# Asking for the convolution's taps first, straight to 128 partitions

## The chip, the cores and the metric

The kernel runs on one core of one Trainium2 chip. The metric is the device time of one execution in microseconds (us): the median of the runs of one kernel. Below, TensorE is the matrix engine (PE for its matmuls, PEld for its weight loads), VectorE is DVE, ScalarE is ACT, GpSimd is POOL, and SyncE is SP. ACT, SP and POOL can also ask for DMA transfers; all of these share the core's 16 DMA engines.

## The reference

Two layers. The first is a causal convolution along the sequence with softmax-normalised taps: 8 heads of 24 channels, 7 taps each. The second is a feed-forward layer with a ReLU gate.

```python
B, S, D = 8, 4096, 192;  H, K = weight.shape      # 8 heads, 7 taps
w = exp(weight - max(weight, axis=-1));  w = w / (sum(w, axis=-1) + 1e-9)
out[b, s, h, :] = sum over k of w[h, k] * x[b, s + k - 6, h, :]      # zero ahead of the sequence
x = out.reshape(32768, 192)
gate = maximum(x @ moe_w_gate, 0);  val = x @ moe_w_val              # 192 -> 1536
result = (gate * val) @ moe_w_out                                     # 1536 -> 192
```

## The kernel before, in words

**Tiles and units.** The batch of 8 sequences is cut into two halves ("streams"), worked side by side: channels 64c to 64c + 63 (c = 0, 1, 2) of stream 0 lie in partitions 0 to 63 and those of stream 1 in 64 to 127. A unit is 1024 tokens of both streams; there are 16 units, each two windows of 512 tokens. For each window, `gate_val` runs over 12 slices f of 128 hidden channels: matmuls with `Wg` and `Wv` (L560), a ReLU on ACT (L571), a product on DVE (L572). `project_turn` then does the last matmul with `Wo` (L582).

**The convolution** is done in two ways. For units 2 to 15, a "lane" of products and sums on ACT, DVE and POOL makes `xc`, using `tap`, a table with one column of 7 taps for each channel. For units 0 and 1 there is no time for that, so TensorE does it: a band matrix per head, 118 rows by 112 tokens, with the 7 taps on its diagonals. `conv_steps` (L372 to L394) takes the first 512 tokens in five steps jj of 112 tokens, for each of the three channel groups c.

**The start**, with which the change is concerned, runs in this order:
- `early` (L129) makes ACT load its exponential table.
- `w8` (L131) asks for the taps as an 8 x 7 tile on ACT's queue. `load_raw` asks for the five blocks of x: jj = 1, 0, 3, 4 on SP's queue, jj = 2 on ACT's (L132 to L134).
- POOL makes `ones`, then by affine selects `rows8` (1 where partition h belongs to head h's 16 columns, L156) and the identity `eye` (L158), then clears `Z` and the first rows of x block 0.
- DVE sums `eye` into `Z` (L164: which of 16 offsets within a head a partition stands for) and `mask` (L170: which head it belongs to). A one-element memset of `Wg` on DVE (L180) is what POOL's first weight request waits for.
- TensorE runs matmuls on constants (`hold`, L195) whose results nobody reads, in counts of 128 columns from `WARM`. Between them stands one matmul of value, L205: `rows8` by `w8` gives `spread`, the taps of head p // 16 in each of 128 partitions. Three matmuls by zeros (L211) clear the PSUM areas in which the bands will be built.
- From `spread`: the negated maximum `mx` on DVE (L285), the exponential `e` on ACT (L288), its sum `sm` (L291), then `prod`, `blk`, the reciprocal and `blocks` on DVE (L297 to L309). Eight matmuls for each of three groups of heads (L330) lay the blocks on the diagonals, and DVE copies the bands out (L338).
- ACT casts the five blocks of x to 16 bits (L121), in the order 1, 0, 2, then the normalised taps `wn` (L318), then 3, 4. They feed the convolution (L386) with the bands; `evict` (L397) writes `xc` for the first 512 tokens, and L560 begins.

**The weights** come by eight requests on POOL's queue (`load_w`, L226: columns cut at 128, 384, 768), into partitions 0 to 63. The upper half is a copy of the lower (`both_halves`, L233), slice by slice: 0 and 1 by DVE, 2 to 9 by POOL (`pool_halves`), 10 (the last 256 columns) by DMA. POOL's queue holds, in this order: the eight requests, copies of slice 2, a load of x, slices 3 to 5, a load of x, slices 6 and 7, a load of x, slices 8 and 9.

**The order of work** on each engine is that of the program text (`manual_schedule`), and each engine takes its queue in order. `psum` has four buffers, used in rotation; `spread` takes one of them. The table `tap` is filled by 20 small DMAs on SP's queue from `wn` (L349), which reads 8 partitions that hold the taps of head h: before, 16h to 16h + 7.

Of the kernel before, what the change touches and what calls it, by code (L numbers as in the profile page):

```python
# [8 lines left out]
FP = mybir.dt.float32  # L9
F16 = mybir.dt.float16  # L10
ACTF = mybir.ActivationFunctionType
ALU = mybir.AluOpType
# [3 lines left out]
def kernel(  # L16
# [12 lines left out]
    nc = tc.nc  # L29

    B, S, D = x.shape
    H, KW = weight.shape
# [10 lines left out]
    STEPS = [6, 5, 2]  # L43
    TAPS = [(6, 5), (4, 3), (2, 1, 0)]
    GSUB = 5
    WARM = [(4, 4, 4, 1), (4, 4, 1)]
    STEPS0 = [1, 0, 2, 3, 4]
    CONV1 = 10

# [12 lines left out]
    const = ctx.enter_context(tc.tile_pool(name="const", bufs=1))  # L62
# [7 lines left out]
    psum = ctx.enter_context(tc.tile_pool(name="psum", bufs=4, space=bass.MemoryType.PSUM))  # L70
# [37 lines left out]
    def load_raw(queue, jj):  # L108
        lo = SUB * jj - PAD
        p0 = max(0, -lo)  # L110
        queue.dma_start(
            out=raw[jj][p0 : ROWS[jj], :].rearrange("p (s d) -> p s d", s=2),
            in_=bass.AP(
                tensor=x.tensor,
                offset=x.offset + (lo + p0) * D,
                ap=[[D, ROWS[jj] - p0], [NB * S * D, 2], [1, D]],
            ),
        )
# [7 lines left out]
    HR = 128 // H  # L126
    BW = HR + PAD
    early = const.tile([128, 1], FP)
    nc.scalar.activation(out=early[:], in_=nc.const_aps.tensor(0.0, [128, 1], FP), func=ACTF.Exp)  # L129
    w8 = const.tile([H, KW], FP)  # L130
    nc.scalar.dma_start(out=w8[:], in_=weight)  # L131
    for jj in (1, 0, 3, 4):  # L132
        load_raw(nc.sync, jj)
    load_raw(nc.scalar, 2)  # L134

    zeros = const.tile([128, 128], F16)
    nc.vector.memset(zeros[:], 0.0)
    e = const.tile([128, KW + 1], FP)
# [5 lines left out]
    def select(out, n, pattern):  # L144
        nc.gpsimd.affine_select(
            out=out,
            in_=ones[0:n, :],
            pattern=pattern,
            compare_op=ALU.is_equal,
            fill=0.0,  # L150
            base=0,
            channel_multiplier=1,
        )

    rows8 = const.tile([H, 128], FP)
    select(rows8[:], H, [[-1, H], [0, HR]])  # L156
    eye = const.tile([128, 128], FP)
    select(eye[:], 128, [[-1, 128]])  # L158
    Z = const.tile([128, 256], F16)
# [3 lines left out]
    with nc.allow_low_precision("one of the terms is not zero"):  # L163
        nc.vector.tensor_reduce(  # L164
            out=Z[:, 112 : 112 + HR],
            in_=eye[:].rearrange("p (g i) -> p i g", i=HR),
            axis=mybir.AxisListType.X,
            op=ALU.add,
        )
    nc.vector.tensor_reduce(  # L170
        out=mask[:, :, 0],
        in_=eye[:].rearrange("p (g i) -> p g i", i=HR),
        axis=mybir.AxisListType.X,
        op=ALU.add,
    )
# [8 lines left out]
    def none(reps, n):  # L184
        z = zeros[:, 0:1]
        return bass.AP(tensor=z.tensor, offset=z.offset, ap=[z.ap[0], [0, reps], [1, n]])
# [3 lines left out]
    def many(n):  # L190
        return bass.AP(tensor=one.tensor, offset=one.offset, ap=[one.ap[0], [0, n]])

    def hold(*counts):
        for reps in counts:
            nc.tensor.matmul(  # L195
                out=held[:, 0, 0 : 128 * reps],
                lhsT=many(128),
                rhs=many(128 * reps),
                start=True,
                stop=True,  # L200
            )

    spread = psum.tile([128, 2, 512], FP, name="ps")
    hold(*WARM[0])
    nc.tensor.matmul(out=spread[:, 0, 0:KW], lhsT=rows8[:], rhs=w8[:], start=True, stop=True)  # L205
    hold(*WARM[1])
    BANDS = [range(0, 3), range(3, 6), range(6, H)]
    raised = [psum.tile([128, 2, 512], FP, name="ps") for _ in range(2)]
    raised = [raised[0][:, 0, :], raised[1][:, 0, :], held[:, 1, :]]
    for part, heads in zip(raised, BANDS):  # L210
        nc.tensor.matmul(  # L211
            out=part[:, 0 : SUB * len(heads)],
            lhsT=zeros[:],
            rhs=none(len(heads), SUB),
            start=True,
            stop=False,
# [14 lines left out]
    def both_halves(copy, s, dst):  # L231
        cols = slice(HALVES[s], HALVES[s + 1])
        copy(out=dst[64:128, :, cols], in_=dst[0:64, :, cols])  # L233
# [46 lines left out]
    for s in (8, 9):  # L280
# [2 lines left out]

    mx = const.tile([128, 1], FP)
    nc.vector.tensor_reduce(  # L285
        out=mx[:], in_=spread[:, 0, 0:KW], axis=mybir.AxisListType.X, op=ALU.max, negate=True
    )
    nc.scalar.activation(out=e[:, 0:KW], in_=spread[:, 0, 0:KW], func=ACTF.Exp, bias=mx[:])  # L288
    sm = const.tile([128, 1], FP)
    total = const.tile([128, KW + 1], FP)  # L290
    nc.scalar.activation(out=total[:], in_=e[:], func=ACTF.Copy, accum_out=sm[:])  # L291
    for jj in STEPS0[:3]:
# [5 lines left out]
        out=prod[:],  # L298
        in0=bass.AP(tensor=z0.tensor, offset=z0.offset, ap=[z0.ap[0], [1, BW], [1, KW]]),
        in1=bass.AP(tensor=e0.tensor, offset=e0.offset, ap=[e0.ap[0], [0, BW], [1, KW]]),  # L300
        op=ALU.mult,
# [5 lines left out]
    for heads in BANDS:  # L307
        n = len(heads)
        nc.vector.scalar_tensor_tensor(  # L309
            out=blocks[:, heads[0] : heads[0] + n, :],  # L310
# [6 lines left out]
    wn = const.tile([128, KW], FP)  # L317
# [5 lines left out]
    for part, heads, to, copy in zip(  # L323
# [3 lines left out]
        for j in range(128 // HR):  # L327
# [3 lines left out]
                out=part[:, 0 : SUB * n].rearrange("p (h t) -> p h t", t=SUB)[:, :, s0 + lo : s0 + hi],  # L331
                lhsT=Z[:, 112 - HR * j : 240 - HR * j],
                rhs=blocks[:, heads[0] : heads[0] + n, lo:hi],
                start=False,
                stop=(j == 128 // HR - 1),
# [6 lines left out]
    for c in range(NCH):  # L342
        r0 = 0
        while r0 < 64:
            h = (64 * c + r0) // G
            r1 = min(64, G * (h + 1) - 64 * c)
            row = wn[HR * h : HR * h + 8, :]
            for st in range(2):
                nc.sync.dma_start(  # L349
                    out=tap[64 * st + r0 : 64 * st + r1, c, :],  # L350
                    in_=bass.AP(
                        tensor=row.tensor,
                        offset=row.offset,
                        ap=[row.ap[0], [0, (r1 - r0) // 8], [1, KW]],
                    ),
                )
            r0 = r1
        if c == 0:
            both_halves(nc.sync.dma_start, 10, Wg)
            both_halves(nc.sync.dma_start, 10, Wv)  # L360
# [290 lines left out]
    for c, copy in enumerate((nc.scalar.copy, nc.vector.tensor_copy, nc.scalar.copy)):  # L651
# [7 lines left out]
        out=plain.rearrange("p (c d) -> p c d", d=D), in_=moe_w_out.rearrange("(c p) d -> p c d", p=128)  # L659
# [92 lines left out]
```

## Time and profile before

| What | Value |
| --- | --- |
| median of 3 runs | 763.53 us (763.51 to 763.62) |
| profiled execution, first to last instruction (its span) | 761.2 us |
| the median's distance from that span | 2.33 us |
| TensorE matmuls | busy 757.1 us, 99% of the span |
| DVE, ACT, POOL | 669.9, 604.0, 425.0 us |
| mean granted TensorE clock | 0.999 |

For the profiled execution the profile gives its span; the time of a run also holds what lies around it. Rows of the order of time have start, length, engine, line, operation, output and inputs, and, in brackets, how long the engine stood idle ahead of it and what ended that. "x4" after a row counts merged instructions. SPq, ACTq and POOL rows named DMA are requests; the transfers run later. Busy matmul time has modelled ends.

### The profile page before, as it was taken

Reading aid. Unit: us, or ns where it says so; the run is one execution under the profiler, and the core shown is the slowest. Engines: PE = TensorE matmul, PEld = TensorE weight load, DVE = VectorE, ACT = ScalarE, POOL = GpSimd, SP = SyncE. Lnnn points to the kernel's source line nnn. Section 1 sums busy time; section 2 is a strip of 40 time slices with the busy share of each in tenths; the row PEclk is TensorE's granted clock in tenths of the full one; section 3 lists DMA queues with packets and bytes.
Section 4 is the critical chain, followed back from the end, with each engine's and each line's share of the span. In section 5 each row is a group of like instructions: output and inputs, shape, how many; then the busy total and the mean of one; then the engine's idle time right before and its main releaser. Section 6 shows DMA issues by size and latency. Waiting matters only on the chain.

```text
span 761.2 us, 30408 instructions
## 1 busy us (share of the span) xinstructions
PE 757.1 (99%) x13732; PEld 497.5 (65%) x13732; DVE 669.9 (88%) x634; ACT 604.0 (79%) x671; POOL 425.0 (56%) x200
## 2 busy tenths in 40 slices
PE   9999999999999999999999999999999999999998
PEld 5556666666666666666666666666666666666668
DVE  7879989998998989989899899998999989896691
ACT  7898887878878788787877878788797887874471
POOL 8608749094591936829277391864909558092000
PEclk9999999999999999999999999999999999999999
DMA  9927536054450534516255152442715432030302
GB/s 149 154 56 131 85 82 86 5 121 49 95 76 6 126 42 98 72 27 119 28 106 65 48 102 23 111 59 70 88 14 121 49 88 42 3 84 3 86 3 84
DMA packets 154513, 54.36 MB, mean 71 GB/s; under 512 B 149632, under 2 KB 154384, under 8 KB 154384
## 3 DMA queue, kind: packets, MB, share of 16 engines
q1 hardware_dynamic: 117600, 37.87, 22.6%
q0 software_dynamic: 36352, 14.26, 17.1%
q8 instruction: 107, 1.75, 0.9%
q10 hardware_dynamic: 432, 0.30, 0.1%
q14 instruction: 22, 0.18, 0.1%
HBM read 29.40 MB, written 25.17 MB: 72 GB/s over the span
## 4 chain that ended last, share of the span: by engine, by line
PE 99%; DMA 0%; ACT 0%; issue 0%
PE ps L560 65%; PE ps L582 31%; PE ps L625 2%; PE ps L386 0%; PE ps L409 0%; DMA w<-in_weight_dram 0%; PE ps L195 0%; PE ps L330 0%; PE ps L211 0%; PE ps L205 0%; ACT out_s L636 0%; ACT L129 0%
## 5 line engine op out<-in xcount | busy, mean ns | idle before, releaser
L572 DVE TENSOR_TENSOR hT<-gr,ps 128x1024 f16<-128x1024 f16 (+1 forms) x385 | 468.9, 1218 | 35.3 <-ACT gr L571 8.3
L571 ACT ACTIVATE gr<-ps 128x1024 f16<-128x1024 f32 (+1 forms) x385 | 392.8, 1021 | 116.5 <-PE ps L560 116.5
L499 POOL TENSOR_TENSOR prod<-prod,prod 128x1792 f32<-128x1792 f32 x70 | 279.5, 3993 | 258.6 <-DVE prod L531 230.8
L560 PE MATMUL ps<-xc,Wg 64*64 64x512 f16 (+1 forms) x4464 | 324.3, 376 | 0.0
L560 PE MATMUL ps<-xc,Wv 64*64 64x512 f16 (+1 forms) x4464 | 324.2, 376 | 0.0
L582 PE MATMUL ps<-hT,Wo 64*64 64x512 f16 x4320 | 236.3, 376 | 0.0
L560 PEld LDWEIGHTS <-Wg 64*64 64x64 f16 (+1 forms) x4464 | 163.5, 107 | 85.2
L560 PEld LDWEIGHTS <-Wv 64*64 64x64 f16 (+1 forms) x4464 | 157.0, 106 | 91.4 <-DVE hT L572 0.3
L582 PEld LDWEIGHTS <-Wo 64*64 64x64 f16 x4320 | 153.9, 107 | 78.9 <-issue 0.3
L490 ACT ACTIVATE prod<-x_r,tap 128x1024 f32<-128x1024 f16 (+1 forms) x182 | 175.1, 1044 | 0.0
L521 DVE SCALAR_TENSOR_TENSOR acc<-x_r,tap,acc 128x1024 f32<-128x1024 f16 (+1 forms) x140 | 113.2, 874 | 2.0 <-ACT acc L510 2.0
L600 DVE STREAM_TRANSPOSE out_s<-ps 128x1024 f32<-128x1024 f32 x45 | 56.1, 1247 | 33.3 <-PE ps L582 28.8
L499 POOL TENSOR_TENSOR xc<-prod,prod 128x1792 f16<-128x1792 f32 x14 | 56.0, 4001 | 0.4
L462 POOL COPY x_p<-x_e 128x1536 f16<-128x1536 f16 x28 | 40.3, 1463 | 0.1
L250 POOL DMA_DIRECT2D x_e<-in_x_dram x28 | 25.5, 911 | 0.0
L595 ACT COPY turned_by<-ps 128x2 f32<-128x2 f32 x45 | 7.0, 156 | 21.8 <-PE ps L582 19.9
L521 DVE SCALAR_TENSOR_TENSOR xc<-x_r,tap,acc 128x1024 f16<-128x1024 f16 (+1 forms) x28 | 24.1, 859 | 0.0
L510 ACT ACTIVATE acc<-x_r,tap 128x1024 f32<-128x1024 f16 (+1 forms) x28 | 21.6, 821 | 0.0
L625 PEld LDWEIGHTS <-hT 128*128 128x128 f16 x192 | 15.8, 98 | 0.4 <-issue 0.4
L625 PE MATMUL ps<-Wo,hT 128*128 128x192 f16 x192 | 16.0, 246 | 0.0
L636 ACT COPY out_s<-ps 128x768 f32<-128x768 f32 (+2 forms) x5 | 3.2, 638 | 12.7 <-PE ps L625 12.7
L636 DVE COPY out_s<-ps 128x192 f32<-128x192 f32 x1 | 0.4, 356 | 13.3 <-PE ps L625 13.3
(58 smaller groups left out, 72.4 us busy)
## 6 DMA issues: line engine op xcount, KB each, us to landing
out_dram<-out_s SPq DMA_DIRECT2D x121, 192.0 KB
x_e<-in_x_dram POOLq DMA_DIRECT2D x28, 384.0 KB, 5.3
x_r<-x_p SPq DMA_TRANSPOSE x112
out_dram<-out_s SPq DMA_DIRECT2D x3, 384.0 KB
out_s<-in_x_dram POOLq DMA_DIRECT2D x4, 240.0 KB, 6.7
prod<-in_moe_w_out_dram POOLq DMA_DIRECT2D x1, 576.0 KB, 9.1
prod<-in_x_dram SPq DMA_DIRECT2D x2, 192.0 KB
out_s<-in_x_dram POOLq DMA_DIRECT2D x2, 192.0 KB, 4.9
```

The source lines that it names most:

```text
L250: nc.gpsimd.dma_start(out=xe[:, :, st, :, :].rearrange("p j c r -> p j (c r)"), in_=bass.AP(tensor=x.tensor, offset=x.offset + row * D, ap ...
L462: nc.gpsimd.tensor_copy(out=xp[:, :, :, st, :], in_=xe[:, :, st, :, :])
L490: nc.scalar.activation(out=prods[u, k][:, at - LDVE : at - LDVE + n], in_=shifted(u, c, k, t, n), func=ACTF.Copy, scale=tap[:, c, k : k + 1],)
L499: nc.gpsimd.tensor_tensor(out=p0[:] if k < KW - 1 else flat(u)[:, LDVE:FLAT], in0=p0[:], in1=prods.pop((u, k))[:], op=ALU.add,)
L510: nc.scalar.activation(out=accs[u][:, at : at + n], in_=shifted(u, c, 0, t, n), func=ACTF.Copy, scale=tap[:, c, 0:1],)
L521: nc.vector.scalar_tensor_tensor(out=(flat(u) if k == KW - 1 else acc)[:, at : at + n], in0=shifted(u, c, k, t, n), scalar=tap[:, c, k : k ...
L560: nc.tensor.matmul(out=pss[i][q : q + M, st, :], lhsT=W[64 * st : 64 * st + 64, c, 128 * f + q : 128 * f + q + M], rhs=xcb[64 * st : 64 * ...
L571: nc.scalar.activation(out=gr[:, sts], in_=pss[0][:, sts], func=ACTF.Relu)
L572: nc.vector.tensor_tensor(out=h[:, f, sts], in0=gr[:, sts], in1=pss[1][:, sts], op=ALU.mult)
L582: nc.tensor.matmul(out=ps[64 * st : 64 * st + 64, b, :], lhsT=Wo[64 * r : 64 * r + 64, f, p, :], rhs=hs[b][64 * r : 64 * r + 64, f, st, :] ...
L600: nc.vector.transpose(out=o[:].rearrange("p t (b d) -> p b t d", b=2)[:, :, :, 32 * p : 32 * p + 32], in_=ps[:].rearrange("p b (t c) -> p ...
L625: nc.tensor.matmul(out=ps[:, i // 2, D * (i % 2) : D * (i % 2) + D], lhsT=h[:, f, st, 128 * q : 128 * (q + 1)], rhs=Wo[:, f, :, :].rearran ...
```

## The change

Four things, all in the start:
- `wrow` takes the place of `w8`: the first request on SP's queue reads the 8 x 7 taps 16 times over into a 128 x 7 tile, head h in partitions h, h + 8, h + 16 and so on. `mx` and `e` read it directly.
- `rows8`, its select on POOL and the matmul L205 go. The PSUM buffer of `spread` is still taken in the rotation. The constant matmuls run in one stretch of 21 x 128 columns instead of 13 and 9.
- `Z`, `mask` and the reads for `tap` follow the new order of heads (head p % 8 instead of p // 16).
- x blocks 1 and 2 are asked for on ACT's queue, and 0, 3, 4 on SP's behind the taps; before, block 2 came on ACT's behind the taps, and 1, 0, 3, 4 on SP's.

```diff
-    WARM = [(4, 4, 4, 1), (4, 4, 1)]
+    WARM = (4, 4, 4, 4, 4, 1)
...
-    w8 = const.tile([H, KW], FP)
-    nc.scalar.dma_start(out=w8[:], in_=weight)
-    for jj in (1, 0, 3, 4):
+    wrow = const.tile([128, KW], FP)
+    nc.sync.dma_start(
+        out=wrow[:],
+        in_=bass.AP(tensor=weight.tensor, offset=weight.offset, ap=[[0, HR], [KW, H], [1, KW]]),
+    )
+    for jj in (0, 3, 4):
         load_raw(nc.sync, jj)
-    load_raw(nc.scalar, 2)
+    for jj in (1, 2):
+        load_raw(nc.scalar, jj)
...
-    rows8 = const.tile([H, 128], FP)
-    select(rows8[:], H, [[-1, H], [0, HR]])
     eye = const.tile([128, 128], FP)
     select(eye[:], 128, [[-1, 128]])
...
             out=Z[:, 112 : 112 + HR],
-            in_=eye[:].rearrange("p (g i) -> p i g", i=HR),
+            in_=eye[:].rearrange("p (i g) -> p i g", i=HR),
...
         out=mask[:, :, 0],
-        in_=eye[:].rearrange("p (g i) -> p g i", i=HR),
+        in_=eye[:].rearrange("p (i g) -> p g i", i=HR),
...
-    spread = psum.tile([128, 2, 512], FP, name="ps")
-    hold(*WARM[0])
-    nc.tensor.matmul(out=spread[:, 0, 0:KW], lhsT=rows8[:], rhs=w8[:], start=True, stop=True)
-    hold(*WARM[1])
+    psum.tile([128, 2, 512], FP, name="ps")
+    hold(*WARM)
...
-        out=mx[:], in_=spread[:, 0, 0:KW], axis=mybir.AxisListType.X, op=ALU.max, negate=True
+        out=mx[:], in_=wrow[:], axis=mybir.AxisListType.X, op=ALU.max, negate=True
     )
-    nc.scalar.activation(out=e[:, 0:KW], in_=spread[:, 0, 0:KW], func=ACTF.Exp, bias=mx[:])
+    nc.scalar.activation(out=e[:, 0:KW], in_=wrow[:], func=ACTF.Exp, bias=mx[:])
...
-            row = wn[HR * h : HR * h + 8, :]
+            row = wn[h : h + 1, :]
...
-                        ap=[row.ap[0], [0, (r1 - r0) // 8], [1, KW]],
+                        ap=[[H * row.ap[0][0], 8], [0, (r1 - r0) // 8], [1, KW]],
```

## The prediction

> **What bounds the kernel now.** I read the page first, then the chain of work that ended last in order of time, then the order of time of the first 20 us, then the busy time in half microseconds.
>
> ```profile
> PE 757.1 (99%) x13732; PEld 497.5 (65%) x13732; DVE 669.9 (88%) x634; ACT 604.0 (79%) x671; POOL 425.0 (56%) x200
> ```
>
> TensorE is busy for 757.1 of 761.2 us. The chain says the same with the order of the pieces:
>
> ```profile
> 0.86 1.56 DMA w<-in_weight_dram
> 2.42 0.14 issue
> 2.56 0.56 PE ps L205 x2
> 3.12 1.07 PE ps L195 x3
> 4.19 0.75 PE ps L211 x3
> 4.93 1.05 PE ps L330 x24
> 5.99 1.60 PE ps L386 x120
> 7.59 13.17 PE ps L560 x120
> ...
> 711.04 31.08 PE ps L560 x576
> ```
>
> The columns are start, length, and what ran. From 7.59 us on, the chain is TensorE alone; whatever the change does happens ahead of that or in the first unit, and later pieces only shift. So the question is how far the stream of L560 is shifted, and whether anything downstream is tied to absolute time and takes the shift back. The ceiling of any gain is small: even the whole DMA, wait and spreading matmul (0.86 to 3.12) is 2.3 us, 0.3%.
>
> **The change part by part.** The start before, in order of time:
>
> ```profile
> 0.86 0.59 ACTq L131 DMA_DIRECT2D w<-in_weight_dram  x1
> ...
> 1.08 0.34 POOL L145 TENSOR_SCALAR_AFFINE_SELECT rows<-ones 8x128 f32<-8x128 f32 x1
> 1.39 0.28 POOL L145 TENSOR_SCALAR_AFFINE_SELECT eye<-ones 128x128 f32<-128x128 f32 x1
> ...
> 2.46 0.06 DVE L180 MEMSET Wg<- 1x1 f16 x1
> ...
> 2.83 0.85 POOL L226 DMA_DIRECT2D Wg<-in_moe_w_gate_dram  x1 [0.55 <-DVE Wg L180]
> ...
> 3.15 0.17 DVE L285 TENSOR_REDUCE mx<-ps 128x1 f32<-128x7 f32 x1 [0.64 <-PE ps L205]
> ...
> 3.86 1.32 ACT L121 CAST out_s<-prod 128x384 f16<-128x384 f32 x3
> ...
> 4.77 1.22 PE L330 MATMUL ps<-blocks,Z 128*128 128x48 f16 x24
> ...
> 5.29 0.91 ACT L121 CAST out_s<-prod 128x384 f16<-128x384 f32 x2
> ```
>
> *The taps.* Before, 8 rows of 28 bytes are asked for at 0.86 and have landed at 2.42; the matmul runs to 3.12 and `mx` starts at 3.15. After, `mx` waits for the DMA itself. SyncE asks 0.05 us earlier, but for 128 rows instead of 8. No row shows that shape. Lower bound: DVE's own queue (two reductions, then the memset that ends at 2.52) is free 0.31 us earlier because POOL loses the first select (start to start 1.39 − 1.08), so 2.21. Upper bound: the first x block, 256 rows of 768 bytes asked for at the same time, had landed when its cast ran at 3.86. I take 2.50, by the nearest row: the 2.42 of the same 224 bytes, plus about 0.08 for more rows and for the semaphore. So `mx` comes 0.65 us earlier. Behind `mx` on DVE stand `prod`, `blk` and `blocks`, behind `e` on ACT the casts; both queues held them back in the same order before.
>
> *From `mx` to the bands.* Same instructions, same lengths: exp, product, sums, blocks. The 24 matmuls of L330 start at 4.77 − 0.65 = 4.12 and the first convolution (L386) at 5.99 − 0.65 = 5.34 by the chain's counting.
>
> *TensorE's clock takes half of that.* What the convolution costs depends on how fast the array runs at that moment:
>
> ```profile
> L330 PE MATMUL ps<-blocks,Z x24: 182/218/247, 4.8 to 5.8; 128*128 128x66 f16 x12, 128*128 128x44 f16 x6, 128*128 128x48 f16 x2, 128*128 128x18 f16 x2
> ```
>
> These forms add up to 1188 columns for the 22 matmuls listed, in 1.05 us: some 1.1 to 1.2 columns per ns. The three zero matmuls (336, 336 and 224 columns, 0.75 us) give 1.19. L560 gives 120 x 512 columns, two at a time, in 13.17 us: 2.33. L386, four at a time on 112 columns, gives 30 x 112 in 1.60: 2.1, with waits in it. So the rate doubles just about when L386 begins, near 5.9 us. The page's row of the granted clock doesn't show it:
>
> ```profile
> PEclk9999999999999999999999999999999999999999
> ```
>
> If that moment stays where it is, the convolution runs from 5.34 to 5.99 at half rate and does 0.33 us worth of its work in 0.65: of the 0.65 us, 0.33 are left, and L560 starts at 7.26 instead of 7.59.
>
> The Trainium skill, page "TensorE: Matmul & The Clock Gate", Part 1, says that the half-rate start is a gate that opens after a busy window of about 3.4 us, and that the windows run freely, not from the kernel's first matmul. By that rule an earlier convolution doesn't bring an earlier clock, and the sum is the 0.33 just taken; without any rule, with the clock tied to the convolution, it would be 0.65. The trace has one doubling in it and can't tell the two.
>
> *The x blocks.* Blocks 1 and 2 now come from ScalarE's queue, 0, 3 and 4 from SyncE's behind the taps. Each queue issues in the same places as before (two on ACT, four on SP), and the bytes are the same, so landings stay where they are, give or take 0.1 us. The engines are full while x moves:
>
> ```profile
> 2.50:3.00 0.50, 0.44 (x2) 0.47 (x2) 0.02 (x2) 0.00 (x0) 0.17 (x1) 1.00 1.01 310
> ...
> 4.50:5.00 0.50, 0.50 (x7) 0.38 (x6) 0.50 (x3) 0.50 (x2) 0.50 (x2) 1.00 1.11 302
> 5.00:5.50 0.50, 0.50 (x14) 0.50 (x12) 0.23 (x2) 0.50 (x3) 0.50 (x1) 1.00 1.07 83
> ```
>
> (The last two columns are the DMA share and GB/s.) The rate falls at 5.0 us: x is through about then, so the casts can't follow the taps by 0.65. The last cast ends at 6.20 now (5.29 + 0.91); I leave it there. Channel group 0 needs it after 48 of the 120 matmuls, at 5.99 + 48/120 x 1.60 = 6.63 before and 6.30 after: no new wait, 0.10 us of room. That caps the start's gain at 0.43.
>
> *The weights.* They decide what arrives at the end. In the first unit the upper half of each weight slice is copied by POOL, and two of these copies end just as TensorE wants them:
>
> ```profile
> 6.15 0.63 POOL L226 DMA_DIRECT2D Wv<-in_moe_w_val_dram  x1
> ...
> 11.39 0.50 POOL L233 COPY Wv<-Wv 64x384 f16<-64x384 f16 x1 [1.01 <-DMA Wv<-in_moe_w_val_dram]
> ...
> 11.92 0.09 PEld L560 LDWEIGHTS <-Wv 64*128 64x128 f16 x1
> ...
> 12.16 0.82 PE L560 MATMUL ps<-xc,Wv 64*128 64x512 f16 x6
> ...
> 17.24 0.52 POOL L233 COPY Wg<-Wg 64x384 f16<-64x384 f16 x1
> ...
> 17.77 0.55 PEld L560 LDWEIGHTS <-Wg 64*128 64x128 f16 x6
> ...
> 17.99 0.83 PE L560 MATMUL ps<-xc,Wg 64*128 64x512 f16 x6
> ```
>
> ```profile
> Wv<-in_moe_w_val_dram POOLq DMA_DIRECT2D x1, 144.0 KB, 5.2
> ```
>
> The 144 KB request for `Wv` is issued at 6.15 and takes 5.2 us, so it lands at 11.35; its copy ends at 11.89, and from there POOL works without a break to 17.76. The matmuls behind the second copy start at 17.99, with the load normally 0.22 us ahead; a waiting load can start its matmul almost at once, so this place gives 17.99 − 17.78 = 0.21 us and no more, unless the weights land earlier by some s. POOL's first request moves forward by 0.31 (the select). But the DMA engines are full, so s lies between 0 and 0.31; I take 0.1, nearer to 0:
>
> ```profile
> 8.50:9.00 0.50, 0.50 (x8) 0.27 (x6) 0.20 (x1) 0.14 (x1) 0.50 (x3) 1.00 1.36 155
> ```
>
> The cap is then 0.31 us.
>
> *At nothing*, for these rows:
>
> ```profile
> 0.84 1.55 PE L195 MATMUL ps<-const-bfloat16-1.0 128*128 128x512 bf16 x4 [0.84 <-PEq L736]
> ...
> 3.05 1.14 PE L195 MATMUL ps<-const-bfloat16-1.0 128*128 128x512 bf16 x3
> ...
> 3.98 0.95 PE L211 MATMUL ps<-zeros 128*128 128x336 f16 x3
> ```
>
> ```profile
> 43.00 1.59 ACT L510 ACTIVATE acc<-x_r,tap 128x1024 f32<-128x1024 f16 x2
> ```
>
> The 21 instead of 22 warming blocks of 128 columns and the missing fp32 matmul cost nothing, since TensorE waits for the blocks at 4.12 anyway: 9 warming blocks took 3.98 − 3.05, so 0.103 each, and 21 of them from 0.84 with the zero matmuls' 0.75 end at 3.76. The tap DMAs from every eighth partition move the same 28-byte rows, and `tap` is first read at 43.00 (if that cover failed, the lane of unit 2 would slip by what they slip). Nor do the new strides of the two reductions: they lie in the 0.29 us that DVE now has between 2.21 and 2.50.
>
> Sum: min(0.33, 0.31), so 0.3 us off the span: 761.2 − 0.3 = 760.9. The median of the runs stands 2.33 us above the profiled span (763.53 − 761.2); I leave that as it is: **763.2 us**.
>
> **The rivals.**
> 1. *The clock comes later (slower).* Before, TensorE's only pause early on ended at 2.56, and the doubling came 3.36 us later. After, the new pause lies between 3.76 and 4.12. If the 3.36 us run from the end of the pause, the doubling comes at 7.48: the convolution does 1.07 of its 1.60 us by then (2.14 at half rate) and ends at 8.01, 0.42 late: 763.95. If it slips by a whole 3.4 us instead, to 9.3, the convolution takes 3.2 us (to 8.54) and L560 loses 0.37 more: +1.32, 764.85. It decides once the blocks come later than 3.76, which is taps landing after about 2.1. For it: the pause sits ahead of the convolution. Against: the earlier stretch had a pause and a thin fp32 matmul (0.56 us for 2 x 7 columns), and the clock came all the same.
> 2. *Nothing arrives.* Weights don't move (s = 0), or x's tail is pushed back by the earlier weights, or the taps land at 2.9 to 3.1. Gain 0 to 0.1: 763.45 to 763.6. For it: DMA share above 1.0 throughout.
> 3. *All of it arrives.* The unbroken warming from 0.84 lets the clock come before 5.34; x's last cast is then the limit (0.43), and the weights move by their full 0.31 (cap 0.52): 763.1; with a faster x, 762.9.
> 4. *The rows are slow.* 128 requests on one 224-byte place land like x, near 3.8: +0.7, 764.2. The change then doesn't do what it says.
>
> **How the numbers follow.** Forecast 0.50 (own range 763.0 to 763.45), rival 1 0.20, rival 2 0.17, rival 3 0.08, rival 4 0.05. The range 762.9 to 764.2 holds the forecast, rivals 2, 3 and 4 and the smaller half of rival 1. A change of 0.2%, about what a measurement of this kernel can tell from none, is 1.53 us: faster than 762.0 would need almost the whole tap path to vanish with no limit behind it (0.03); slower than 765.06 needs rival 1 at its worst and something beside it (0.05); within, 0.92.
>
> **What would show it.** In the changed kernel: `mx` at about 2.5; L330 from about 4.1; L386 from about 5.3 with its first groups at half the pace; the last cast still ending near 6.2; L560 from about 7.25; the load of slice 8 waiting for POOL's copy; then pieces of 31.08 as before. It is wrong if `mx` starts after 2.9, if L386 takes over 2.2 us (rival 1), or if POOL's copy of the fourth `Wv` slice starts at 11.39 again or later (rival 2).

## The result, and the profile after

| | before | after |
| --- | --- | --- |
| median (lowest to highest) | 763.59 us (763.35 to 764.71), 14 runs | 765.80 us (764.71 to 766.21), 14 runs |
| ratio, with its 95% interval | | 1.0026 (1.0019 to 1.0032) |
| span of the profiled execution | 761.2 us | 764.3 us |

The changed kernel is slower by 2.2 us, or 0.29% of the medians. The profiled execution is one of its longer ones (766.04 us). In it the span is 3.1 us longer than before. The chain that ended last (start, length, what ran) holds all of it:

```profile
0.81 3.31 DMA wrow<-in_weight_dram
4.11 0.02 issue
4.14 0.17 DVE mx L285
...
5.78 1.21 PE ps L330 x24
6.99 2.68 PE ps L386 x110
9.67 14.19 PE ps L560 x120
23.86 1.54 PE ps L386 x119
```

Set beside the same pieces of before: the taps land at 4.11 instead of 2.42, although no matmul stands behind them any more, and `mx` starts 0.99 us later (4.14 against 3.15). In the order of time L330 starts 1.01 us late (5.78 against 4.77) and takes as long as before (1.21 against 1.22); the chain of before counts it only from 4.93, where the last matmul ahead of it ends. L386 takes 1.08 more and the first 120 matmuls of L560 1.02 more. 1.01 + 1.08 + 1.02 = 3.11. So there are two losses: the taps are **late**, and TensorE is **slow** for longer. The order of time of the start shows both:

```profile
0.81 0.72 SPq L131 DMA_DIRECT2D wrow<-in_weight_dram  x1
...
2.54 0.85 POOL L226 DMA_DIRECT2D Wg<-in_moe_w_gate_dram  x1 [0.57 <-DVE Wg L182]
...
4.14 0.16 DVE L285 TENSOR_REDUCE mx<-wrow 128x1 f32<-128x7 f32 x1 [1.90 <-DMA wrow<-in_weight_dram]
...
5.78 1.21 PE L330 MATMUL ps<-blocks,Z 128*128 128x48 f16 x24 [1.79 <-DVE blocks L309]
5.95 0.92 ACT L121 CAST out_s<-prod 118x384 f16<-118x384 f32 x2 [0.58 <-DMA prod<-in_x_dram]
...
6.98 0.91 ACT L121 CAST out_s<-prod 128x384 f16<-128x384 f32 x2
...
11.09 0.50 POOL L233 COPY Wv<-Wv 64x384 f16<-64x384 f16 x1 [0.21 <-DMA Wv<-in_moe_w_val_dram]
...
11.29 0.64 PE L560 MATMUL ps<-xc,Wg 64*128 64x512 f16 x2
11.71 0.43 PE L560 MATMUL ps<-xc,Wv 64*128 64x512 f16 x2
11.97 0.81 PE L560 MATMUL ps<-xc,Wg 64*128 64x512 f16 x6
```

`mx` waits 1.90 us for the DMA and for nothing else. TensorE waits 1.79 us for the blocks. Two matmuls of L560 take 0.61 to 0.64 us up to 11.29 and 0.43 at 11.71, and six take 0.81 after that: the doubling of the rate that came near 5.9 before comes near 11.8. POOL's side moved as it should: its first request stands at 2.54 instead of 2.83, and the copy of the fourth `Wv` slice at 11.09 instead of 11.39. While the taps trickle in, the DMA engines even have room for half a microsecond: their share is 1.07 from 2.5 to 3.0, 0.76 from 3.5 to 4.0, and between them (the last two columns are DMA share and GB/s):

```profile
3.00:3.50 0.50, 0.50 (x4) 0.33 (x3) 0.00 (x0) 0.00 (x0) 0.50 (x2) 1.00 0.49 148
```

### The profile page after: what moved, and what is told of

Its sections match the earlier page's. It is cut to its first block, busy times and chain, and to the rows that moved or that the text cites. A ratio compares the mean times of both kernels' runs of the same rounds, so it can differ in the third digit from the quotient of the medians.

```text
span 764.3 us, 30401 instructions
## 1 busy us (share of the span) xinstructions
PE 758.6 (99%) x13729; PEld 497.8 (65%) x13729; DVE 670.0 (88%) x634; ACT 604.1 (79%) x671; POOL 424.8 (56%) x199
## 4 chain that ended last, share of the span: by engine, by line
PE 99%; DMA 0%; DVE 0%; ACT 0%; issue 0%
PE ps L560 65%; PE ps L582 31%; PE ps L625 2%; PE ps L386 1%; DMA wrow<-in_weight_dram 0%; PE ps L409 0%; PE ps L330 0%; DVE prod L297 0%; ACT out_s L636 0%; DVE blk L304 0%; ACT e L288 0%; DVE blocks L309 0%; DVE mx L285 0%; DVE sm L305 0%
## 5 line engine op out<-in xcount | busy, mean ns | idle before, releaser
L560 PE MATMUL ps<-xc,Wg 64*64 64x512 f16 (+1 forms) x4464 | 324.9, 376 | 0.0
L560 PE MATMUL ps<-xc,Wv 64*64 64x512 f16 (+1 forms) x4464 | 324.7, 376 | 0.0
L560 PEld LDWEIGHTS <-Wg 64*64 64x64 f16 (+1 forms) x4464 | 163.3, 107 | 85.7 <-issue 0.8
L560 PEld LDWEIGHTS <-Wv 64*64 64x64 f16 (+1 forms) x4464 | 156.9, 106 | 92.3 <-issue 0.7
```

The source lines that it names most:

```text
L560: nc.tensor.matmul(out=pss[i][q : q + M, st, :], lhsT=W[64 * st : 64 * st + 64, c, 128 * f + q : 128 * f + q + M], rhs=xcb[64 * st : 64 * ...
```

## The experiments

Two questions: why are the taps late, and what does lateness cost. The theories on the first: **ORDER** (the rows queue behind x, which ACT asks for at the same time), **PLACE** (many readers of one 224-byte place), **PATTERN** (a source with two row steps, 0 and 7 elements). On the second: the clock, x's casts or the weights. Each edit is shown against the changed kernel, where nothing else is said.

### 1. The taps with no x beside them

```diff
-    for jj in (0, 3, 4):
+    for jj in (1, 0, 2, 3, 4):
         load_raw(nc.sync, jj)
-    for jj in (1, 2):
-        load_raw(nc.scalar, jj)
```

> The changed kernel, with all five blocks of x on SyncE's queue behind the taps (order 1, 0, 2, 3, 4), so that nothing else is asked for until the taps' request is out at about 1.5 us. Theory ORDER (the taps' rows wait behind the 256 rows of x block 1 that ScalarE asks for at the same moment): mx starts at 2.4 to 2.8 instead of 4.14. Theory ROWS (128 rows of 28 bytes are slow by themselves): mx stays at 3.6 or later. In both, x lands up to 1 us later than in the changed kernel, so the total is open: 763.5 to 765 by ORDER, 766 to 767 by ROWS.

Measured: 768.33 us, ratio to before 1.0059 (1.0046 to 1.0072). In the order of time:

```profile
3.91 0.16 DVE L283 TENSOR_REDUCE mx<-wrow 128x1 f32<-128x7 f32 x1 [1.68 <-DMA wrow<-in_weight_dram]
...
7.49 0.51 ACT L121 CAST out_s<-prod 128x384 f16<-128x384 f32 x1 [1.70 <-DMA prod<-in_x_dram]
...
9.46 0.51 ACT L121 CAST out_s<-prod 80x384 f16<-80x384 f32 x1 [0.28 <-DMA prod<-in_x_dram]
```

With no x in front of them or beside them the taps gain 0.23 us (3.91 against 4.14), less than the 0.43 by which two executions with the very same requests differ (4.14 in the changed kernel, 4.57 in experiment 5). As the main cause ORDER falls. It has a share in when the first row moves: between 2.25 and 2.35 us here, between 2.6 and 2.7 in the changed kernel. The new loss is x, five requests behind each other on one queue: its last cast ends at 9.97, and the total is above the range of either theory.

### 2. Only the order of the requests (edit to the kernel before)

```diff
-    nc.scalar.dma_start(out=w8[:], in_=weight)
-    for jj in (1, 0, 3, 4):
+    nc.sync.dma_start(out=w8[:], in_=weight)
+    for jj in (0, 3, 4):
         load_raw(nc.sync, jj)
-    load_raw(nc.scalar, 2)
+    for jj in (1, 2):
+        load_raw(nc.scalar, jj)
```

> The kernel before with only the order of the requests changed: the taps as 8 rows, first on SyncE's queue, x blocks 1 and 2 on ScalarE's, 0, 3, 4 on SyncE's; spreading matmul and warming as before. Theory ROWS: 8 rows are quick from this place too, the spreading matmul at about 2.55, total 763.4 to 763.9, as before. Theory ORDER: the 8 rows too wait behind x block 1, the spreading matmul at 3.2 or later, total 764.3 or more.

> A second look at the kernel before with the new order of requests alone, since the first look fell on one of its longest executions. Theory WEIGHTS: the taps come 0.2 us earlier again, L560 starts 0.1 to 0.2 us earlier, and the gain is lost at the Wv copy of slice 3 or at slice 8, so that the ten slices before L386's second turn end no earlier than in the kernel before (20.76). Theory START ONLY: they end 0.1 to 0.2 us earlier and stay so.

Measured: 763.45 us, ratio 0.9999 (0.9990 to 1.0008). The profiled execution was a longer one (764.48); a second one, profiled alone, took 763.32. Order of time, first execution, then second:

```profile
2.95 0.17 DVE L286 TENSOR_REDUCE mx<-ps 128x1 f32<-128x7 f32 x1 [0.43 <-PE ps L206]
...
13.16 0.50 POOL L234 COPY Wv<-Wv 64x384 f16<-64x384 f16 x1 [2.77 <-DMA Wv<-in_moe_w_val_dram]
```

```profile
5.30 0.95 ACT L121 CAST out_s<-prod 128x384 f16<-128x384 f32 x2
...
9.20 0.28 DVE L234 COPY Wv<-Wv 64x384 f16<-64x384 f16 x1 [1.15 <-DMA Wv<-in_moe_w_val_dram]
```

Eight rows on SP's queue bring `mx` 0.20 us earlier with the matmul still there, and L560 starts 0.15 earlier (7.41 against 7.56; L561 in this kernel). In the second execution its first 120 matmuls still end where they did (20.75 against 20.76): on DVE the copy of slice 1 of `Wv` waits 1.15 us for its DMA, and the products queue behind it. So the order is free, and a start gained by 0.15 is lost to the weights. In the longer execution the fourth slice's copy waited 2.77 us, to 13.16: how late that load lands changes from execution to execution.

### 3. 128 different rows

```diff
-        in_=bass.AP(tensor=weight.tensor, offset=weight.offset, ap=[[0, HR], [KW, H], [1, KW]]),
+        in_=bass.AP(tensor=moe_w_gate.tensor, offset=moe_w_gate.offset, ap=[[DFF, 128], [1, KW]]),
```

> The changed kernel, but the 128 rows of 28 bytes are read from 128 rows of the gate weight, 6 KB apart, instead of 16 times from the 224 bytes of the taps; its taps are therefore not the reference's. Theory PLACE (many reads of one place, or the repeat in the access pattern, are slow): mx at about 2.5, total about 763.4. Theories ROWS and ORDER: mx near 4.1 as in the changed kernel, total 765.3 to 766.2.

> A second look at the changed kernel with 128 different rows 6 KB apart, for the same reason (its taps are not the reference's). mx at 2.7 to 2.8 and L330 from about 4.4 as in the first look. Theory X BLOCKS: the last cast of x ends at 6.5 to 6.7 instead of 6.20, and L560 starts at 7.5 to 7.6 however early the taps are. Theory WEIGHTS ONLY: L560 starts by 7.3 and the gain is lost later.

Measured: 763.58 us, ratio 1.0001 (0.9992 to 1.0010), and 763.26 in a second, single execution. Order of time of the first, then the chain of the second:

```profile
0.81 0.40 SPq L131 DMA_DIRECT2D wrow<-in_moe_w_gate_dram  x1
...
2.74 0.16 DVE L285 TENSOR_REDUCE mx<-wrow 128x1 f32<-128x7 f32 x1 [0.50 <-DMA wrow<-in_moe_w_gate_dram]
...
4.38 0.81 PE L330 MATMUL ps<-blocks,Z 128*128 128x48 f16 x24 [0.45 <-DVE blocks L309]
...
5.35 2.26 PE L386 MATMUL ps<-band,out_s 118*32 118x112 f16 x120 [0.17 <-DVE band L338]
```

```profile
1.74 3.84 DMA prod<-in_x_dram
...
5.60 0.93 ACT out_s L121 x2
...
6.58 0.96 PE ps L386 x72
7.54 13.32 PE ps L560 x120
```

Into the same 128 partitions, by the same queue, as many bytes: `mx` is at 2.74, where the prediction wanted it (2.5, not after 2.9). Neither the 128 rows nor the queue is the trouble. (The edit changes the place and the pattern at once, two row steps to one; experiment 4 parts them.) And yet nothing is won: L386 starts 0.57 us earlier than before (5.35 against 5.92 in the order of time) and ends at the same time, because x is now the limit. In the second execution the last cast ends at 6.53 (5.60 + 0.93), and the last 72 matmuls run from 6.58.

### 4. The source taken apart: pattern, place, distance

Three kernels, each with one line other than the changed kernel, in this order: 128 different rows in two steps; one 28-byte row read 128 times in one step; 128 different rows side by side in one step.

```diff
-        in_=bass.AP(tensor=weight.tensor, offset=weight.offset, ap=[[0, HR], [KW, H], [1, KW]]),
+        in_=bass.AP(tensor=moe_w_gate.tensor, offset=moe_w_gate.offset, ap=[[DFF, HR], [HR * DFF, H], [1, KW]]),
...
+        in_=bass.AP(tensor=weight.tensor, offset=weight.offset, ap=[[0, 128], [1, KW]]),
...
+        in_=bass.AP(tensor=moe_w_gate.tensor, offset=moe_w_gate.offset, ap=[[KW, 128], [1, KW]]),
```

> The changed kernel reading 128 different rows of the gate weight, but through a source pattern of two row steps (16 rows by 8), as the changed kernel's is; its taps are not the reference's. Theory PATTERN (two row steps in the source make SyncE and the generating of requests slow): the request takes 0.72 us on SyncE instead of 0.40, mx at 3.8 to 4.6, total 765.2 to 766.2. Theory PLACE (reading one 224-byte place 16 times is slow): mx at 2.7 to 2.8 as with the other rows, total 763.2 to 763.8.

> The changed kernel with one row step in the source, of 0: all 128 partitions read the same 28 bytes, so every head has the taps of head 0. Theory PATTERN: the request takes 0.40 us on SyncE and mx comes at 2.7 to 2.8, total 763.2 to 763.8. Theory PLACE: mx at 3.8 or later, total 765.2 or more.

> The changed kernel reading 128 different rows of 28 bytes that lie side by side in the gate weight (3.5 KB in all, one row step); its taps are not the reference's. Theory SAME BYTES (what is slow in the one-place read is that all 16 engines read the very same few bytes again and again): mx at 2.7 to 2.9, as with rows 6 KB apart, total 763.2 to 763.9. Theory NEARNESS (small rows within a few KB of each other are slow, whether the same or not): mx at 3.5 or later, total 764.8 or more.

| source | request | rows move | `mx` starts | time | ratio |
| --- | --- | --- | --- | --- | --- |
| the change: 8 rows, 16 times, two steps | 0.72 | 2.63 to 3.80 | 4.14 | 765.80 | 1.0026 (1.0019 to 1.0032) |
| two steps, all different | 0.72 | 2.62 to 2.98 | 3.47 | 765.55 | 1.0027 (1.0017 to 1.0036) |
| one place, one step | 0.40 | 1.82 to 3.81 | 4.18 | 765.48 | 1.0028 (1.0017 to 1.0040) |
| different rows 6 KB apart, one step | 0.40 | 1.82 to 2.37 | 2.74 | 763.58 | 1.0001 (0.9992 to 1.0010) |
| different rows side by side, one step | 0.40 | 1.82 to 2.25 | 2.61 | 763.35 | 0.9993 (0.9984 to 1.0003) |

"Rows move" is from the first to the last of the 128 packets of 28 bytes in the trace, one execution each. Ratios are to the kernel before as measured in the same comparison (763.48 to 764.13 us), so the times of two rows can't be set against each other.

PATTERN and PLACE are both true, and one of them is enough to be late. They act at different ends, as the packets between 1.6 and 2.1 us show; "under 512 B" counts the 128 rows and the semaphore writes. The lines are of the changed kernel, of experiment 3 and of one place, in that order:

```profile
DMA packets 11, 0.01 MB, mean 17 GB/s; under 512 B 0, under 2 KB 11, under 8 KB 11
```

```profile
DMA packets 131, 0.01 MB, mean 19 GB/s; under 512 B 123, under 2 KB 131, under 8 KB 131
```

```profile
DMA packets 24, 0.00 MB, mean 1 GB/s; under 512 B 24, under 2 KB 24, under 8 KB 24
```

Different rows in one step are nearly through by 2.1. With two steps the first row hasn't started: the request itself takes 0.72 us instead of 0.40, and no small packet is seen up to 2.6 either. From one place the rows start on time and then come slowly. So two steps cost 0.80 us at the start (2.62 against 1.82), and one place stretches the moving from about 0.5 us to between 1.2 and 2.0. Part of the 0.80 is order after all: in experiment 1, also with two steps but no x asked beside them, the rows start at 2.28. Between 2.1 and 2.6 us, experiment 1 and then the changed kernel:

```profile
DMA packets 34, 0.00 MB, mean 2 GB/s; under 512 B 34, under 2 KB 34, under 8 KB 34
```

```profile
DMA packets 126, 0.10 MB, mean 194 GB/s; under 512 B 0, under 2 KB 126, under 8 KB 126
```

Why one place is slow is not settled: whether the memory or the engines make its readers wait was not tried.

The two-step run also shows the second loss: its `mx` is only 0.32 us later than before, and it is as slow as the changed kernel. Order of time, then half rate in the windows (the third column from the right is the granted clock):

```profile
5.11 0.81 PE L330 MATMUL ps<-blocks,Z 128*128 128x48 f16 x24 [1.13 <-DVE blocks L309]
6.09 0.28 PE L386 MATMUL ps<-band,out_s 118*32 118x112 f16 x8 [0.17 <-DVE band L338]
6.82 0.93 ACT L121 CAST out_s<-prod 118x384 f16<-118x384 f32 x2 [2.11 <-DMA prod<-in_x_dram]
...
7.38 3.06 PE L386 MATMUL ps<-band,out_s 118*32 118x112 f16 x112 [1.01 <-ACT out_s L121]
```

```profile
0.85:4.26 3.41, 3.13 (x9) 1.23 (x10) 1.12 (x7) 1.99 (x6) 2.76 (x7) 1.00 0.62 156
4.26:7.68 3.42, 1.37 (x40) 1.03 (x39) 2.32 (x9) 1.31 (x5) 3.42 (x6) 1.00 1.18 186
7.68:11.09 3.41, 3.26 (x108) 2.36 (x110) 1.67 (x5) 2.25 (x6) 2.35 (x5) 0.50 1.10 164
```

L330 already runs at the full rate here (0.81 us for what takes 1.21 in the changed kernel). Then TensorE waits for an x block, asked for at 1.58 behind the rows and landed at 6.74, and from 7.68 the clock is 0.50 for 3.41 us: gained, and lost again. This holds for the profiled execution (766.43 us); in 7 of the 10, the median among them, the mean clock is 1.000, so what makes the median slow is not shown by this trace.

### 5. The pause filled

```diff
-    WARM = (4, 4, 4, 4, 4, 1)
+    WARM = (4, 4, 4, 4, 4, 4, 4, 4, 4, 4, 1)
```

> The changed kernel with 41 instead of 21 warming blocks of 128 columns, so that TensorE is busy until about 5.8 us, when the blocks come. Theory CLOCK (the pause from 3.77 to 5.78 puts off the doubling of the rate, which costs about 2 of the 3.1 us): L386 takes about 1.6 instead of 2.68 us, L560 starts near 8.7, total 764.3 to 764.8. Theory LATE TAPS ALONE (the whole loss comes from late taps and late x): L386 stays above 2.4 us and the total at 765.3 to 766.2.

Measured: 764.53 us (764.26 to 764.85), ratio 1.0011 (1.0003 to 1.0020). Order of time, then the chain:

```profile
4.57 0.16 DVE L285 TENSOR_REDUCE mx<-wrow 128x1 f32<-128x7 f32 x1 [2.33 <-DMA wrow<-in_weight_dram]
...
6.21 0.81 PE L330 MATMUL ps<-blocks,Z 128*128 128x48 f16 x24 [1.01 <-DVE blocks L309]
```

```profile
7.18 1.68 PE ps L386 x119
8.89 13.20 PE ps L560 x120
```

The taps land later still, and the kernel is faster, as CLOCK said. L386 is back at 1.68 and the first 120 matmuls of L560 at 13.20. Each kernel set beside its own before, 765.80 − 763.59 = 2.21 us fall to 764.53 − 763.48 = 1.05. So **about 1.2 of the 2.2 us are the clock** (2.21 − 1.05 = 1.16), and the **1.05 that stay are the late taps**; by its interval that part is 0.2 to 1.5 us.

### 6. No warming at all (edit to the kernel before)

```diff
-    WARM = [(4, 4, 4, 1), (4, 4, 1)]
+    WARM = [(), ()]
```

> The kernel before without its 22 warming blocks; TensorE has only the spreading matmul at 2.56, the zero matmuls and then L330. Theory CLOCK BY ACTIVITY (the rate doubles some 3.4 to 4 us after TensorE's work becomes unbroken, wherever that is): the doubling moves from 5.9 to between 7.5 and 8.5, L386 takes about 3 instead of 1.6 us, total 764.5 to 765.5. Theory FIXED MOMENT (the doubling is tied to the start of the kernel): L386 as before, total 763.3 to 763.8.

Measured: 764.13 us, ratio 1.0007 (0.9998 to 1.0017). The chain:

```profile
4.58 1.22 PE ps L330 x24
5.79 2.71 PE ps L386 x116
8.50 13.94 PE ps L560 x118
```

L386 takes 2.71 us, as in the changed kernel, without any late taps: the clock alone does that. The profiled execution is the longest of ten (764.83), with the doubling at 10.10 by the clock's records, against 5.88 in the kernel before: FIXED MOMENT falls. CLOCK BY ACTIVITY has the direction, but neither its moment (7.5 to 8.5) nor its total (764.5 or more). In the median, warming nothing costs 764.13 − 763.57 = 0.56 us, which the interval can't tell from none.

### 7. Room for the weights (experiment 2 and a finer cut)

```diff
-    CUTS = [0, 128, 384, 768, DFF]
+    CUTS = [0, 128, 384, 512, 768, DFF]
...
-    for s in range(4):
+    for s in range(5):
```

> The kernel before with the new order of requests (8 rows of taps first on SyncE, x blocks 1 and 2 on ScalarE) and with the third pair of weight requests cut in two (columns 384 to 511, 512 to 767), so that slice 3 comes in 48 KB requests of its own. Theory WEIGHTS (in the run with the new order alone the 0.2 us gained by the taps were lost, with 1 us more, at the Wv copy of slice 3): the copy of slice 3 ends before 11.5 us, the wait of 1.0 us there goes, and the total is 763.0 to 763.3, below the kernel before. Theory NO ROOM (the DMA engines are full, cutting only moves the wait): 763.4 or more.

Measured: 763.68 us, ratio 1.0002 (0.9993 to 1.0011). L561 starts at 7.40, and its first 120 matmuls end at 20.92, later than the 20.76 of before; the copies of slice 3 end at 12.07, against 11.89. The cut gives POOL two more requests of 0.63 us each ahead of its copies; NO ROOM holds for this way of making some.

### The clock, by its own records

The traces record when TensorE's clock changed. In the two-step run that is at 4.26, 7.68 and 11.09, in experiment 1 at 4.61, 8.03 and 14.85: multiples of 3.41 us apart. Where this grid lies against the start differs by execution. The table takes stretches of this grid, with TensorE's busy time in each by the windows view, and the clock that followed:

| run | stretch | PE busy us | clock after it |
| --- | --- | --- | --- |
| before | 2.47 to 5.88 | 3.32 | full |
| the change | 1.56 to 4.98 | 2.43 | half |
| the change | 4.98 to 8.39 | 2.61 | half |
| the change | 8.39 to 11.80 | 3.41 | full |
| 1, taps alone | 1.20 to 4.61 | 2.79 | full |
| 1, taps alone | 4.61 to 8.03 | 1.19 | half (lost) |
| 1, taps alone | 8.03 to 11.44 | 2.54 | half |
| 3, first execution | 0.32 to 3.73 | 2.89 | full |
| 3, second execution | 0.07 to 3.48 | 2.64 | full |
| 3, second execution | 3.48 to 6.90 | 2.52 | full (kept) |
| 4, two steps | 4.26 to 7.68 | 1.37 | half (lost) |
| 4, one place | 2.81 to 6.22 | 1.57 | half |
| 4, side by side | 2.91 to 6.33 | 3.16 | full |
| 5, pause filled | 4.09 to 7.50 | 2.22 | full (kept) |
| 6, no warming | 3.28 to 6.69 | 2.62 | half |

With the clock at half, every stretch with 2.62 us or less (77%) left it there, and every one with 2.64 or more gave the full clock; the traces not listed agree. The two are 0.02 us apart and the ends of matmuls are modelled, so the bar lies near three quarters and no finer. Once given, the clock was kept at 2.22 (65%) and lost at 1.37 (40%). Behind the last matmuls the same grid narrows this: kept after 1.88 us (55%, the change, 759.32 to 762.73), lost after 1.42 (42%, experiment 3, 758.08 to 761.49). Three rows of the changed kernel's windows, with PE busy as the second number:

```profile
1.56:4.98 3.42, 2.43 (x8) 0.99 (x7) 1.05 (x5) 1.34 (x6) 2.85 (x6) 1.00 0.73 209
4.98:8.39 3.41, 2.61 (x92) 2.58 (x95) 2.75 (x11) 2.33 (x6) 2.84 (x6) 1.00 1.30 177
8.39:11.80 3.41, 3.41 (x76) 1.93 (x66) 1.36 (x3) 1.17 (x2) 2.93 (x6) 1.00 1.06 152
```

The pause from 3.98 to 5.78 falls on two stretches and spoils both. The granted clock stands at 1.00 in all three rows although the array runs at half rate: the view knows no clock ahead of the first record, so there only the lengths of the matmuls tell. The Trainium skill, page "TensorE: Matmul & The Clock Gate", Part 1, has a window of 3413 ns that runs free of the kernel's start, so that the number of slow matmuls varies from run to run. The records agree to the hundredth of a us. The Trainium skill's table in the same part lets the clock fall after an idle window; here it fell after windows that were 35% and 40% busy, with no pause of TensorE over 1.57 us, and the measurement decides.

It also fits the spread of the changed kernel: in 6 of its 14 executions the mean clock is 0.998, which is one stretch at half rate after a first grant (0.5 x 3.41 / 764 = 0.002), and in the other 8 it is 1.000. That the rest of its spread (1.50 us, against 0.59 with the pause filled) is the place of the grid is argued, not shown.

## Why the prediction was wrong

**Where it failed: the taps.** The step took a landing of 2.42 plus 0.08 "by the nearest row" and got 4.11. The nearest row was that of the same 224 bytes read once by eight rows. What counted was how they are read: with different rows in one step 128 rows land for an `mx` at 2.61 to 2.74, as the step said; read from one place, 4.18; in two steps, 3.47. Even the upper bound was too low (3.86, by x): x has all its rows in different places and its 128 partitions in one step (a second step runs over the two streams).

**Two rivals came at once.** Rival 4 (the rows land like x, +0.7, 764.2) was half of the mechanism, and too small: `mx` came 0.99 late, and lateness cost 1.05. It named one of the two causes, "128 requests on one 224-byte place", with a chance of 0.05; the two row steps, which alone put `mx` at 3.47, it did not name. Late taps then opened the pause of rival 1, which I had priced only for taps that come in time: 0.42 to 1.32 us, measured about 1.2. Added up, the two prices give 763.53 + 0.7 + 0.42 to 1.32, so 764.65 to 765.55: most of the way to 765.80, and outside the range that held them one by one.

**Rival 1's rule was wrong in kind.** It let the doubling follow the pause by 3.36 us, "once the blocks come later than 3.76". In experiment 3 the blocks came at 4.38 and the clock had come at 3.73, ahead of the pause. What fits every record is the busy share of a stretch on a grid. The forecast's own premise, that the doubling stays near 5.9, fell too: it came at 11.80 in the changed kernel, and between 3.48 and 6.33 where the taps were in time and TensorE warmed. That an earlier convolution by itself brings no earlier clock is in line with the records.

**"At nothing"** for the pause between 3.76 and 4.12 held for a pause of that size (0.45 us in experiment 3) and not for the 1.79 us that came. (The matmuls on constants and zeros end at 3.99, not 3.76.)

**The x blocks.** "Landings stay where they are, give or take 0.1": with the new order and eight rows the last cast ends at 6.25 to 6.42 (experiments 2 and 7), with 128 rows ahead on SP's queue at 6.53 to 6.61 (experiment 3 and near rows), against 6.20 before. The cap of 0.43 us that I had put on the start was in fact about nothing: with `mx` 0.41 and 0.54 us early, L560 started at 7.54 to 7.60, against 7.59. So the forecast's gain of 0.3 would not have come with taps in time either: rival 2 would have been right, with ratios of 1.0001 and 0.9993 that can't be told from 1.

**The weights.** POOL's requests moved by 0.29 (0.31 predicted). The cap was real and tighter than 0.21 + s: what experiment 2 gained (0.15) was lost at slice 1 already, ahead of the two places that the prediction had priced.

**Right:** `mx` to L330 and all that stands behind the first unit are unchanged, the reads for `tap` and the strides cost nothing that shows, and the signs that were to show it wrong (`mx` after 2.9, L386 over 2.2 us) did.

No version beat the kernel before: the best, near rows, stands at 0.9993 (0.9984 to 1.0003), which can't be told from none, and it doesn't load the taps.

## What to carry to other kernels

Size a DMA by a row with the same source pattern, not by its bytes: reading one small place into many partitions cost 1.4 to 1.6 us more here than different rows did. When two rivals hang on the same number, price them together. Ahead of the first full clock a pause of TensorE can be paid twice, as lateness and as a stretch at half rate: fill it until the work arrives, and see what else is due at the same time before counting the gain.

## What the hardware showed that I had not expected

- A source of two row steps took SP 0.72 us to ask for, one of one step 0.40, with 128 rows in both; the first row moved 0.80 us later (2.62 against 1.82), 0.35 of it only with x asked beside it, and `mx` came 0.73 later (3.47 against 2.74).
- 128 rows of 28 bytes from one place: `mx` at 4.18; side by side: 2.61.
- The clock was gained with TensorE idle for nearly a quarter of the stretch (busy 2.64 of 3.41 us), kept at 55% busy and lost at 42%.
- The 144 KB load of `Wv` landed for a copy at 13.16 in one execution of experiment 2 and by 11.32 in the other; the long executions of the kernel before (to 765.4 us) may be of that kind, which no profile of that kernel shows.
